# A GEGLU feed-forward layer by Strassen-Winograd: what is loaded beside x's first half, and where four bf16 products stand

## The chip, the cores and the metric

The kernel runs on one core of a Trainium2 chip. A time is the device time of one execution in microseconds; the time before is the median of three runs, 276.03 us (275.87 to 276.15). One further execution was profiled; it took 276.09 us. The engines are TensorE (PE in the profile; PEld is its weight load), VectorE (DVE), ScalarE (ACT), GpSimd (POOL) and SyncE (SP); SP and ScalarE issue the DMAs (SPq, ACTq).

## The reference

```python
def _gelu(x):
    return jax.nn.gelu(x, approximate=True)
def reference(x, w_gate, w_up, w_down):
    return (_gelu(x @ w_gate) * (x @ w_up)) @ w_down
```

x is 32 x 32 x 1024 (1,024 rows of D = 1,024), w_gate and w_up are 1,024 x 3,584, w_down is 3,584 x 1,024, all bf16.

## The kernel before

Every one of the three matrix products is cut in 2 x 2 and done with seven products instead of eight (the Winograd form of Strassen's scheme). The seven products are P1 to P7 in the code's names: `first_products`, `second_products` and so on. In stage 1 the two by two are w_gate's and w_up's columns against the two halves of D (the a's), and x's row halves against the halves of D (the B's: B11 and B21 are the two D halves of the first 512 rows, B12 and B22 those of the last 512, all transposed while they are loaded). F is walked in 28 blocks of 128 columns. P1 and P2 of a block use weights and x as they are loaded, in bf16; the other five use sums of them (S1 to S4, T1 to T4), kept as fp32r. A product is four matmuls of 128 x 128 by 128 x 512.

P1 and P2 of a block together give the gate of the first 512 rows. P1's result is also copied out by ScalarE (E1) and later seeded into another PSUM bank (X), into which P6, P7 and P4 are added in turn: P6, a copy of X by ScalarE (E2), P7, another copy (e3), P4. P5 and P3 go into Y. VectorE makes U1 from Y and e3, H1 from Y and E2, and multiplies gelu's output with them into gT, the input of stage 2. Because the copies are taken between products that go into the same bank, P7 of a block has to wait for the block's E2, and P4 for its e3.

All of this is written out by hand (`tc.manual_schedule()`): each engine and each queue takes its work in the order of the code. The order around the change is this:

- SP starts the transposing load of B11 (L131). ScalarE issues the first part of w_gate tile 0 (L132: the first two of eight row groups of D), then a dummy gelu that brings the activation table in.
- TensorE does ten warm-up products on a constant (L139). Behind the fourth (n = 3) ScalarE copies a few elements and issues three more parts (tile 0's row groups 2 and 3, and the first halves of tiles 1 and 2). Behind the ninth it writes a few elements into B21's place (L147). SP's load of B21 (L148) has to wait for that write, and all later loads of SP stand behind it, in this order: tile 3's first half, the second halves of tiles 0 to 2, half of w_up's first tile, tile 3's second half, tile 4, x's last 512 rows (L155, transposed), tile 5 (L156), the other half of w_up's first tile.
- TensorE: P1 of blocks 0 to 7, P2 of blocks 0 to 7, P1 of 8 and 9, P2 of 8 and 9 (blocks 2c and 2c + 1 use w_gate tile c). Then P5 of blocks 0 and 1 as a pair, P1 of block 10 (`first_products(LEAD)`), P6 of the pair, P1 of block 11, P7 of the pair, P2 of block 10, and P4 and P3 of block 0 and of block 1.
- VectorE: the sums of blocks 0 and 1 as soon as w_up is there, T1 to T4 as soon as x's last 512 rows are there, U1 of blocks 0 and 1 (L258), the sums of block 2, and then the gT and H1 of blocks 0 and 1.
- The loop (L318) then takes one block at a time: P6, the previous block's P4, P5, `ahead()` in most turns, P7, the previous block's P3. `ahead()` does one more P1 and P2 of later blocks; the first call does P1 of block 12 and P2 of block 11.

Stage 2 (L351 on) does the same with gT and w_down. Its last product is the sum of 14 matmuls for each of four row tiles (L502); ScalarE copies each result to SBUF (L506) and it is stored, the last store being issued on ScalarE's own queue.

Of the kernel before, what the change touches and what calls it, by code (L numbers as in the profile page):

```python
# [7 lines left out]
ACT = mybir.ActivationFunctionType  # L8
# [4 lines left out]
def kernel(  # L13
# [18 lines left out]
    nc = tc.nc  # L32
# [10 lines left out]
    DT = D // P  # L43
    KH = DT // 2
    FT = F // P
    NT = N // P
    DB = 512
# [3 lines left out]
    LEAD = 10  # L51
    ALONE = (4, 7, 10, 13, 16, 19, 22, 25)
    KF = FT // 2
    TT = NT // 2
# [28 lines left out]
    def load_gate(c, queue, lo=0, hi=DT):  # L83
        if c not in WG:
            WG[c] = gw.tile([P, DT, 2 * P], bf16, name="gw", tag="gw")
        queue.dma_start(
            out=WG[c][:, lo:hi, :], in_=wg_r[:, lo:hi, 2 * c * P : (2 * c + 2) * P]
        )

    def load_up(c, lo=0, hi=4):  # L90
        if c not in WU:
            WU[c] = uw.tile([P, DT, 4 * P], bf16, name="uw", tag="uw")
        nc.sync.dma_start(
            out=WU[c][:, :, lo * P : hi * P],
            in_=wu_r[:, :, (4 * c + lo) * P : (4 * c + hi) * P],
        )
# [4 lines left out]
    def a11(i):  # L101
        return block(WG, 2, i, 0)

    def a12(i):
        return block(WG, 2, i, 1)
# [18 lines left out]
    def psum_p(name):  # L124
        return psum.tile([P, NB], fp32, name=name, tag="p")

    def psum_q(name):
        return psum.tile([P, NB], fp32, name=name, tag="q")

    with tc.manual_schedule():  # L130
        nc.sync.dma_start_transpose(out=B11, in_=xf[0:NB, 0 : KH * P])  # L131
        load_gate(0, nc.scalar, 0, 2)  # L132
        ones = nc.const_aps.tensor(1.0, [P, NB], bf16)
        warm = [psum_p("warm") for _ in range(4)]
        table = opool.tile([P, 8], bf16, name="table", tag="o")
# [1 line left out]

        for n in range(NWARM):
            nc.tensor.matmul(warm[n % 4], lhsT=ones[:, 0:P], rhs=ones, start=True, stop=True)  # L139
            if n in (3, 8):  # L140
                nc.scalar.activation(table, warm[n % 4][:, 0:8], ACT.Copy)
            if n == 3:
                load_gate(0, nc.scalar, 2, KH)
                load_gate(1, nc.scalar, 0, KH)
                load_gate(2, nc.scalar, 0, KH)
            if n == 8:
                nc.scalar.activation(B21[:, 0, 0:8], table, ACT.Copy)  # L147
# [5 lines left out]
        load_gate(3, nc.sync, KH, DT)  # L153
        load_gate(4, nc.sync)
        nc.sync.dma_start_transpose(out=xt1, in_=xf[NB:N, :])  # L155
        load_gate(5, nc.sync)  # L156
        load_up(0, 2, 4)

        T = {}
# [13 lines left out]
        def early_sums(i, engine=nc.gpsimd):  # L173
            S1[i], S3[i] = weight_tile("s1"), weight_tile("s3")
            engine.tensor_tensor(S1[i], a21(i), a22(i), ALU.add)  # L175
            engine.tensor_tensor(S3[i], a11(i), a21(i), ALU.subtract)  # L176
# [14 lines left out]
        def pair_product(ps, lhs, rhs, first, cuts):  # L191
            for lo, hi in zip(cuts, cuts[1:]):
                for p, l in zip(ps, lhs):
                    for k in range(lo, hi):
                        nc.tensor.matmul(  # L195
                            p,
                            lhsT=l[:, k, :],
                            rhs=rhs[:, k, :],
                            start=(first and k == 0),
                            stop=(k == KH - 1),  # L200
                            skip_group_check=True,
                        )

        def first_products(*blocks, cuts=(0, KH)):
            for i in blocks:
                A[i] = psum_p("a") if 4 <= i < 8 else psum_q("a")
            pair_product([A[i] for i in blocks], [a11(i) for i in blocks], B11, True, cuts)
            for i in blocks:
                if i % 2 == 0:
                    pool, tag = (xpool, "e1") if i == LEAD - 2 else (ring, "ring")  # L210
                    E1[i // 2] = pool.tile([P, 2, NB], fp32, name="e1", tag=tag)
                nc.scalar.activation(E1[i // 2][:, i % 2, :], A[i], ACT.Copy)  # L212

        def second_products(*blocks, cuts=(0, KH)):
            pair_product([A[i] for i in blocks], [a12(i) for i in blocks], B21, False, cuts)
            for i in blocks:
                if i % 2 == 0:
                    GL[i // 2] = half.tile([P, 2, NB], bf16, name="gl0", tag="half")
                nc.scalar.activation(GL[i // 2][:, i % 2, :], A[i], ACT.Gelu_apprx_tanh)

        X, Y, E2, U1, G1 = {}, {}, {}, {}, {}
# [5 lines left out]
        done = LEAD + 2  # L227

        def ahead():
            nonlocal done  # L230
            if done < FT:
                first_products(done)
            second_products(done - 1)
            done += 1

        def sixth_products(*blocks):
            cuts = range(0, KH + 1, 2)
            pair_product([X[i] for i in blocks], [S2[i] for i in blocks], T["T2"], False, cuts)
            for i in blocks:
                E2[i] = epool.tile([P, NB], fp32, name="e2", tag="e2")  # L240
                nc.scalar.activation(E2[i], X[i], ACT.Copy)  # L241
# [9 lines left out]
        def seventh_products(*blocks):  # L251
            cuts = range(0, KH + 1, 2)
            pair_product([X[i] for i in blocks], [S3[i] for i in blocks], T["T3"], False, cuts)
            for i in blocks:
                e3 = epool.tile([P, NB], fp32, name="e3", tag="e3")
                nc.scalar.activation(e3, X[i], ACT.Copy)  # L256
                U1[i] = epool.tile([P, NB], bf16, name="u1", tag="u1")
                nc.vector.tensor_tensor(U1[i], Y[i], e3, ALU.add)  # L258
# [28 lines left out]
        copy_a22(0)  # L287
        second_products(8)
        second_products(9)
        for k in range(KH):  # L290
            nc.scalar.activation(T["B22"][:, k, :], B22[:, k, :], ACT.Copy)
        copy_a22(1)
# [2 lines left out]
        pair_product(  # L295
            [Y[0], Y[1]], [S1[0], S1[1]], T["T1"], True, range(KH + 1)
        )
        first_products(LEAD)
        sixth_products(0, 1)
        first_products(LEAD + 1)  # L300
        seventh_products(0, 1)
        second_products(LEAD)
        early_sums(2, nc.vector)
        second_sum(2)
        seed(2)
# [12 lines left out]
        for i in range(2, FT + 1):  # L318
# [16 lines left out]
            if here and i not in ALONE and done <= FT:  # L335
                ahead()
# [55 lines left out]
        def step(ps, lhs, rhs, j, t, first=False, last=False):  # L392
            for i in range(2):
                nc.tensor.matmul(  # L394
                    ps,
                    lhsT=lhs[:, i, t * P : (t + 1) * P],
                    rhs=rhs[:, i, :],
                    start=(first and j == 0 and i == 0),
                    stop=(last and j == JF - 1 and i == 1),
                    skip_group_check=True,  # L400
                )
# [9 lines left out]
        X = [psum.tile([P, DB], fp32, name="x", tag="p") for t in range(TT)]  # L411
# [90 lines left out]
        for t in range(TT):  # L502
            for j in range(JF):
                step(X[t], SC[j], TC[j], j, t, last=True)
            o_sb = opool.tile([P, DB], bf16, name="o_sb", tag="o")
            nc.scalar.activation(o_sb, X[t], ACT.Copy)  # L506
            queue = nc.sync if t < TT - 1 else nc.scalar
            queue.dma_start(out=of[(TT + t) * P : (TT + t + 1) * P, 0:DB], in_=o_sb)

# [29 lines left out]
```

## Time and profile before

| | before |
|---|---|
| median of 3 runs | 276.03 us (275.87 to 276.15) |
| profiled execution | 276.09 us, of which span 274.3 us |
| PE busy | 268.9 us (98%) |
| PEld busy | 189.3 us (69%) |
| DVE busy | 188.6 us (69%) |
| ACT busy | 138.2 us (50%) |
| POOL busy | 87.2 us (32%) |
| granted TensorE clock, mean | 1.000 |
| DMA | 26.42 MB, mean 96 GB/s |

The span runs from the first to the last instruction of the program. The busy time of TensorE is that of matmuls whose ends are modelled and which overlap; where TensorE loses time is read from the distance of their starts, and from the bracket at the end of a timeline row, which gives the engine's idle time before the row and what ended it. Some matmul records are missing in a trace. In a timeline row the columns are the start, the time from start to end, the engine, the line, the operation, what is written and read with the shapes, and the number of instructions taken together. An SPq or ACTq row is the issue of a DMA; its data moves and lands later.

### The profile page before, as it was taken

How to read it: one execution, taken by the hardware profiler on the slowest of the kernel's cores; microseconds unless marked ns; L12 is line 12 of the kernel's file. 1: busy time of each engine (PE TensorE's matmuls, PEld its weight loads, DVE VectorE, ACT ScalarE, POOL GpSimd, SP SyncE). 2: the span in 40 equal slices, each digit the busy share in tenths (PEclk: the TensorE clock that was granted, in tenths of full speed). 3: DMA queues.
4: the chain of work that ended last, by engine and by line, in shares of the span. 5: the costliest groups of instructions: out<-in, count | busy, mean ns of one | idle time of the engine just before them, and what ended most of it. 6: DMA issues, size and time to landing. Idle time of an engine off the chain costs nothing.

```text
span 274.3 us, 3336 instructions
## 1 busy us (share of the span) xinstructions
PE 268.9 (98%) x1172; PEld 189.3 (69%) x1186; DVE 188.6 (69%) x226; ACT 138.2 (50%) x239; POOL 87.2 (32%) x81
## 2 busy tenths in 40 slices
PE   8999999999999999999999999999999999999995
PEld 2445667768777687776877768764447888888883
DVE  0068974866658666686666866769994999999900
ACT  2678565566556665566655666531100072860311
POOL 0000083845558455584555845600000000000000
PEclk9999999999999999999999999999999999999999
DMA  8999402153400034215360202459602000000221
GB/s 174 280 272 269 155 1 76 51 181 103 128 2 0 0 102 131 76 44 187 97 211 0 76 2 77 114 190 327 215 0 76 2 0 0 1 2 0 97 96 38
DMA packets 41008, 26.42 MB, mean 96 GB/s; under 512 B 9248, under 2 KB 40992, under 8 KB 40992
## 3 DMA queue, kind: packets, MB, share of 16 engines
q1 hardware_dynamic: 39248, 25.30, 31.8%
q10 hardware_dynamic: 1744, 0.92, 1.3%
q8 instruction: 9, 0.15, 0.2%
q14 instruction: 7, 0.06, 0.1%
HBM read 22.02 MB, written 2.10 MB: 88 GB/s over the span
## 4 chain that ended last, share of the span: by engine, by line
PE 96%; DMA 2%; issue 0%; ACT 0%
PE x L195 19%; PE x L394 18%; PE y L115 18%; PE a L195 18%; PE x L115 9%; PE y L394 9%; PE z L394 4%; DMA xt<-in_x_dram 2%; PE y L195 1%; ACT o_sb L506 0%
## 5 line engine op out<-in xcount | busy, mean ns | idle before, releaser
L195 PE MATMUL x<-T,s 128*128 128x512 f32 x224 | 63.4, 407 | 0.0
L195 PEld LDWEIGHTS x<-T,s 128*128 128x128 f32 x224 | 41.6, 188 | 10.9 <-ACT e L241 0.3
L195 PE MATMUL a<-xt,gw 128*128 128x512 bf16 x182 | 44.0, 380 | 1.1 <-DMA xt<-in_x_dram 0.5
L184 POOL TENSOR_TENSOR s<-gw,s 128x512 fp32r<-128x512 bf16 x22 | 26.0, 1184 | 48.4 <-PE y L115 47.7
L258 DVE TENSOR_TENSOR u<-y,e 128x512 bf16<-128x512 f32 x28 | 19.3, 691 | 32.0 <-ACT e L256 31.2
L180 DVE TENSOR_TENSOR s<-s,gw 128x512 fp32r<-128x512 f32 x24 | 34.4, 1434 | 0.0
L195 PEld LDWEIGHTS <-gw 128*128 128x128 bf16 x192 | 17.4, 98 | 24.4 <-issue 5.7
L265 ACT ACTIVATE gl<-h 128x512 bf16<-128x512 bf16 x28 | 17.7, 631 | 28.5 <-DVE h L263 28.5
L245 DVE TENSOR_TENSOR gT<-gl,x 128x512 bf16<-128x512 bf16 x28 | 19.2, 687 | 17.9 <-PE x L115 17.9
L115 PE MATMUL x<-T,c 128*128 128x512 f32 x112 | 30.4, 393 | 0.0
L115 PE MATMUL y<-B,s 128*128 128x512 f32 x112 | 30.2, 391 | 0.0
L175 POOL TENSOR_TENSOR s<-uw 128x512 fp32r<-128x512 bf16 x25 | 29.2, 1167 | 0.0
L115 PE MATMUL y<-T,s 128*128 128x512 f32 x104 | 27.8, 389 | 0.0
L394 PE MATMUL x<-tc,sc 128*128 128x512 f32 x112 | 25.7, 389 | 0.0
L212 ACT ACTIVATE e<-a 128x512 f32<-128x512 f32 x28 | 16.6, 597 | 17.2 <-PE a L195 17.2
L256 ACT ACTIVATE e<-x 128x512 f32<-128x512 f32 x28 | 16.7, 600 | 15.7 <-PE x L195 15.7
L176 POOL TENSOR_TENSOR s<-gw,uw 128x512 fp32r<-128x512 bf16 x21 | 24.5, 1166 | 0.0
L115 PEld LDWEIGHTS x<-T,c 128*128 128x128 f32 x112 | 20.9, 188 | 5.1 <-ACT e L256 0.7
L115 PEld LDWEIGHTS y<-B,s 128*128 128x128 f32 x112 | 21.0, 188 | 4.7
L394 PEld LDWEIGHTS x<-tc,sc 128*128 128x128 f32 x112 | 21.0, 188 | 4.4
L115 PEld LDWEIGHTS y<-T,s 128*128 128x128 f32 x104 | 19.5, 188 | 4.1
L394 PEld LDWEIGHTS <-gT 128*128 128x128 bf16 x112 | 10.9, 98 | 13.3 <-issue 0.3
(57 smaller groups left out, 346.9 us busy)
## 6 DMA issues: line engine op xcount, KB each, us to landing
uw<-in_w_up_dram SPq DMA_DIRECT2D x6, 1024.0 KB, 6.3
gw<-in_w_gate_dram SPq DMA_DIRECT2D x8, 512.0 KB, 3.9
v<-in_w_down_dram SPq DMA_DIRECT2D x5, 512.0 KB, 3.5
v<-in_w_down_dram SPq DMA_DIRECT2D x4, 640.0 KB, 8.2
v<-in_w_down_dram SPq DMA_DIRECT2D x8, 256.0 KB, 4.2
out_dram<-o_sb SPq DMA_DIRECT2D x15, 128.0 KB, 1.7
gw<-in_w_gate_dram SPq DMA_DIRECT2D x5, 256.0 KB, 3.9
uw<-in_w_up_dram SPq DMA_DIRECT2D x2, 512.0 KB, 5.7
```

The costliest lines, as they stand in the source:

```text
L115: nc.tensor.matmul(ps, lhsT=lhs[:, k, :], rhs=rhs[:, k, :], start=(first and k == 0), stop=(k == KH - 1), skip_group_check=True,)
L175: engine.tensor_tensor(S1[i], a21(i), a22(i), ALU.add)
L176: engine.tensor_tensor(S3[i], a11(i), a21(i), ALU.subtract)
L180: nc.vector.tensor_tensor(S2[i], S1[i], a11(i), ALU.subtract)
L184: engine.tensor_tensor(S4[i], a12(i), S2[i], ALU.subtract)
L195: nc.tensor.matmul(p, lhsT=l[:, k, :], rhs=rhs[:, k, :], start=(first and k == 0), stop=(k == KH - 1), skip_group_check=True,)
L212: nc.scalar.activation(E1[i // 2][:, i % 2, :], A[i], ACT.Copy)
L245: nc.vector.tensor_tensor(gT[:, i, 0:NB], GL[i // 2][:, i % 2, :], X[i], ALU.mult)
L256: nc.scalar.activation(e3, X[i], ACT.Copy)
L258: nc.vector.tensor_tensor(U1[i], Y[i], e3, ALU.add)
L265: nc.scalar.activation(G1[i], h1, ACT.Gelu_apprx_tanh)
L394: nc.tensor.matmul(ps, lhsT=lhs[:, i, t * P : (t + 1) * P], rhs=rhs[:, i, :], start=(first and j == 0 and i == 0), stop=(last and j == JF ...
```

## The change

There are four edits.

1. ScalarE no longer issues the first part of w_gate tile 0 ahead of its dummy gelu. All four early parts are issued behind the third warm-up (n = 2) instead of three of them behind the fourth.
2. The load of w_gate tile 5 is two DMAs, the first half of D and the second.
3. Four bf16 products change place. P1 of block 10 stands ahead of P5 of blocks 0 and 1 instead of behind it; P1 of block 11 ahead of P6 instead of behind it; P2 of block 10 ahead of P7 instead of behind it; and P2 of block 11, which was in the loop's first `ahead()`, stands between P7 and P4. The first `ahead()` does P1 of block 12 alone.
4. The copy of the last row tile's result is shared: ScalarE takes the first 256 columns and VectorE the last 256. The store, on ScalarE's queue, waits for both.

```diff
         nc.sync.dma_start_transpose(out=B11, in_=xf[0:NB, 0 : KH * P])
-        load_gate(0, nc.scalar, 0, 2)
...
-            if n in (3, 8):
+            if n in (2, 8):
                 nc.scalar.activation(table, warm[n % 4][:, 0:8], ACT.Copy)
-            if n == 3:
+            if n == 2:
+                load_gate(0, nc.scalar, 0, 2)
                 load_gate(0, nc.scalar, 2, KH)
                 load_gate(1, nc.scalar, 0, KH)
                 load_gate(2, nc.scalar, 0, KH)
...
         nc.sync.dma_start_transpose(out=xt1, in_=xf[NB:N, :])
-        load_gate(5, nc.sync)
+        load_gate(5, nc.sync, 0, KH)
+        load_gate(5, nc.sync, KH, DT)
         load_up(0, 2, 4)
...
             if done < FT:
                 first_products(done)
-            second_products(done - 1)
+            if done > LEAD + 2:
+                second_products(done - 1)
             done += 1
...
         second_products(8)
         second_products(9)
+        first_products(LEAD)
...
         pair_product(
             [Y[0], Y[1]], [S1[0], S1[1]], T["T1"], True, range(KH + 1)
         )
-        first_products(LEAD)
+        first_products(LEAD + 1)
         sixth_products(0, 1)
-        first_products(LEAD + 1)
+        second_products(LEAD)
         seventh_products(0, 1)
-        second_products(LEAD)
+        second_products(LEAD + 1)
         early_sums(2, nc.vector)
...
             o_sb = opool.tile([P, DB], bf16, name="o_sb", tag="o")
-            nc.scalar.activation(o_sb, X[t], ACT.Copy)
+            part = DB if t < TT - 1 else DB // 2
+            nc.scalar.activation(o_sb[:, :part], X[t][:, :part], ACT.Copy)
+            if part < DB:
+                nc.vector.tensor_copy(o_sb[:, part:], X[t][:, part:])
             queue = nc.sync if t < TT - 1 else nc.scalar
```

## The prediction

> **What bounds the kernel now.** I read the page first, then the chain of waits, then the timeline of the first 42 us, then what the DMA queues moved.
>
> ```profile
> span 274.3 us, 3336 instructions
> PE 268.9 (98%) x1172; PEld 189.3 (69%) x1186; DVE 188.6 (69%) x226; ACT 138.2 (50%) x239; POOL 87.2 (32%) x81
> PE 96%; DMA 2%; issue 0%; ACT 0%
> ```
>
> TensorE bounds it, and no product is removed. So only three things can move: the DMA 2% at the head of the chain, the places where TensorE waits, and the copy and store behind its last matmul. The head, by the timeline:
>
> ```profile
> 0.74 1.42 SPq L131 DMA_TRANSPOSE xt<-in_x_dram  x1
> 0.74 0.43 ACTq L86 DMA_DIRECT2D gw<-in_w_gate_dram  x1
> 2.76 1.45 ACTq L86 DMA_DIRECT2D gw<-in_w_gate_dram  x3
> ...
> 5.31 2.37 SPq L148 DMA_TRANSPOSE xt<-in_x_dram  x1
> 5.74 2.53 PE L195 MATMUL a<-xt,gw 128*128 128x512 bf16 x11 [0.54 <-DMA xt<-in_x_dram]
> ...
> 11.07 0.98 PEld L195 LDWEIGHTS <-gw 128*128 128x128 bf16 x6 [0.49 <-DMA gw<-in_w_gate_dram]
> ```
>
> The reader sees x's first half landing at 0.74 + 4.96 = 5.70 (the chain's figure) and the first product at 5.74. The wait at 11.07 is for w_gate tile 3's first half. What the DMA engines did meanwhile, 40 slices of 0.2 us from 0 to 8 us:
>
> ```profile
> DMA  0000000002399999249999999997999999999999
> GB/s 0 0 0 0 0 0 0 0 0 74 110 285 238 251 204 64 44 76 276 291 289 289 294 291 295 334 246 172 300 292 292 282 289 294 289 294 256 233 223 291
> ```
>
> Part one of w_gate moves from 1.8, x from about 2.4. From 2.8 to 3.6 the rate collapses (204, 64, 44, 76), with both in flight; then x runs alone at 290. From about 4.8 the other three ScalarE parts follow, until 7.3, where x's second half starts.
>
> The second place is the end of the setup, 31 to 41 us:
>
> ```profile
> 31.40 1.28 DVE L258 TENSOR_TENSOR u<-y,e 128x512 bf16<-128x512 f32 x2
> 35.00 0.68 DVE L263 TENSOR_TENSOR h<-y,e 128x512 bf16<-128x512 f32 x1
> 36.38 0.69 DVE L263 TENSOR_TENSOR h<-y,e 128x512 bf16<-128x512 f32 x1
> 37.11 0.63 ACT L265 ACTIVATE gl<-h 128x512 bf16<-128x512 bf16 x1 [0.76 <-DVE h L263]
> 37.64 0.61 ACT L187 ACTIVATE c<-uw 128x512 fp32r<-128x512 bf16 x1
> 38.16 0.58 ACT L241 ACTIVATE e<-x 128x512 f32<-128x512 f32 x1
> 38.79 1.67 PEld L195 LDWEIGHTS x<-T,s 128*128 128x128 f32 x8 [0.27 <-ACT e L241]
> 40.24 0.61 ACT L256 ACTIVATE e<-x 128x512 f32<-128x512 f32 x1
> 40.89 0.76 PEld L115 LDWEIGHTS x<-T,c 128*128 128x128 f32 x4 [0.43 <-ACT e L256]
> ```
>
> This is an in-order chain: VectorE's u sums at 31.40, nine VectorE instructions to the second h (ends 37.07), its gelu, the copy of C22, the copy of the sixth product, and only then block 2's seventh product at 38.79. VectorE works without a gap from 22.17, when x's second row half has landed, through T1 to T4, to 37.4. So before the change, this chain starts at a DMA.
>
> **The change part by part.** Small losses are taken between matmul starts: 0.216 us apart in bf16, 0.23 in fp32r; where bf16 turns to fp32r one start takes 0.42. The number of such turns does not change.
>
> 1. *x alone.* 512 KB at 290 GB/s are 1.81 us. From 2.4 that is 4.2, and landing trails the last row by 0.66 (5.04 to 5.70), so x lands near 4.9 instead of 5.70. ScalarE's queue loses its first issue (0.43), so the table load moves up from 1.20 to 0.76; the copy behind the third warm-up starts when that product ends, about 2.3, and the four parts issue from 2.3 to 4.2. Part one now stands behind x. Before, the first part behind x landed 0.49 after it (2.76 + 3.43 = 6.19). So part one lands near 5.4, and TensorE starts near 5.43 instead of 5.74: 0.3 earlier. The ten warm-ups end at 5.0 in both.
>
> 2. *The DMA queue behind it.* 128 KB more follow x (0.45 us at 290), x ends 0.8 to 0.87 earlier: ScalarE's parts end 0.3 to 0.4 earlier. x's second half is still issued at 5.31 (it waits for ScalarE's write at L147 behind the ninth warm-up); the first half took 1.63 from issue to first row, so it can't start before 6.9 instead of 7.25. I take the queue 0.3 earlier from there on. From 9 us it is full until past x's last transpose, so everything in it lands 0.3 earlier. Bounds: 0.6 earlier (a shorter latency when nothing is beside), 0.45 later (the collapse stays, and the 128 KB come on top). Tile 3's first half lands at 10.73 instead of 11.03, against 10.62 when TensorE wants it: a wait of 0.1 stays. TensorE then runs 0.3 ahead to about 22.9.
>
> 3. *One product ahead of P5.* Block 10's first product now comes right behind second product 9 and needs w_gate tile 5, which is why that load is cut in two. Whole, it landed at 20.10 + 4.37 = 24.47, or 2.39 behind x's last transpose (22.08). Its first half: at the earliest 1.14 behind, as tile 3's half landed behind x's second half (11.03 against 9.89); at the latest 1.64 (24.47 less 256 KB at the 350 GB/s of that stretch). I take 1.40, between the two rows, which are equally near: 22.08 - 0.3 + 1.40 = 23.18. TensorE is free at 22.9, so it waits 0.3, and the head start of part 1 is spent. Block 10 starts at 23.23. P5 then finds T1 ready; before, it lost 0.27 there.
>
> 4. *Where the seventh products of blocks 0 and 1 now stand.* From block 10's start: first product 0.65, P5 2.06, first 11 0.66, sixth 2.08, second 10 0.66, a turn: 6.13, so 29.36. Before it was 28.72, with one product fewer ahead. The u sum begins 2.4 later, behind the copy e3: 31.76. Before, e3 was ready at 31.09 and VectorE at 31.40. So the chain now starts 0.36 later, at TensorE, and VectorE idles some 0.6 behind T4.
>
> 5. *One product ahead of P4.* Second product 11 leaves block 2's loop turn and stands ahead of P4. P4 waited for nothing (T4 ends 31.48, its first start is 31.45), so nothing is won there; the matmuls between the seventh products and block 2's seventh become one product fewer (second 10 leaves to the front): 9.95 - 0.86 = 9.09 us. The chain over the same stretch is 2.4 + (38.79 - 31.40 = 7.39) = 9.79. TensorE thus waits 0.7 at block 2's seventh product, which starts at 39.15 instead of 38.79: +0.36.
>
> 6. *Given back.* ScalarE no longer has gelu 11 between that product and its copy e3 (0.5 us in its queue, 39.76). The copy then starts as the product ends, and P4 of block 2 loses 0.06 instead of 0.28: -0.22. From there on the order is the old one, and TensorE has no wait until the end.
>
> 7. *The last copy*, 271.00 to 271.60, with the store issued at 271.62.
>
> ```profile
> 271.00 0.60 ACT o_sb L506
> ```
>
> Half on ScalarE, half on VectorE. ScalarE: 8 columns 0.18 to 0.21, 512 columns 0.60, so 256 take 0.39. VectorE: 512 columns from PSUM 0.69, 1,024 of SBUF 1.22, so 256 take 0.42. The store waits for the slower and a semaphore: -0.15 (bounds -0.2 and, if both reads of one bank collide, 0).
>
> Covered: the extra DMA issue on SP (0.58) delays block 2's w_up (lands 26.3, read at 32.60) and tile 6 (29.1, read at 37.1). GpSimd's sums of block 3 start 0.36 later; their S4 of block 2 ended at 38.43 and is read past 45.
>
> Sum: +0.36 - 0.22 - 0.15 = 0.0. The profiled execution took 276.09 (span 274.3 and 1.8 around it), 0.06 above the median 276.03. So 276.05.
>
> A rule weighed: the Trainium skill, "DMA: Bandwidth & Descriptors", section "Queues, rings and completion order", says that each DMA engine goes round between its queues packet by packet. By it, part one, ready near 3.4, would go between x's rows. The row: from 3.8 to 4.8 us, with ScalarE's next parts issued from 2.76, only x's queue moved (1136 packets, all under 512 B), which speaks against it; the collapse at 2.8 to 3.6 speaks for it.
>
> **The rivals.**
>
> *Slower: the collapse stays.* ScalarE's first part becomes ready about 1.1 us after its issue (0.74 to 1.8 before), so near 3.4, in the middle of x's 1.8 us. If its packets go between x's rows, the 0.8 us are lost again and 0.45 us of part one come behind. The queue is then 0.45 later, tile 5's half lands at 23.93, and the chain of part 4 starts 1.1 later than before: 1.11 - 0.22 - 0.15 = +0.74, 276.8. The same happens if x's second half meets the parts' end and collapses instead; before, it met it at 7.2 at no visible price. It decides above a delay of some 0.25. For it: x's last transpose, which started among loads, also fell to 23 GB/s near 18 us. Against: the full rate from 3.8 to 4.8.
>
> *Faster: VectorE's chain has slack.* If the queue gains 0.6 and tile 5's half lands 1.14 behind, part 4 starts at 31.41, and the sum is 0 - 0.22 - 0.15 = -0.37; the full gain, with no wait at block 2's seventh, would be 0.34 there, 0.28 at P4 and 0.15 at the end: 275.3. Against: nine VectorE instructions in order, none of which the change shortens.
>
> *It does not do what it says*: TensorE starts no earlier, as part one lands late. Then parts 3 to 7 still hold, since tile 5 decides: 276.05 to 276.2.
>
> **How the numbers follow.** No change to the end, 276.05 (275.6 to 276.5 for tile 5's two bounds and a queue gain of 0 to 0.6): 0.5, and 0.05 for the rival that does nothing. The collapse: 0.25, 276.5 to 277.1. Faster: 0.2, 275.0 to 275.5. About 0.2% (0.55 us) is what a measurement of this kernel can tell from no change. That gives faster 0.2, same 0.55, slower 0.25, and a range of 275.3 to 276.9, which leaves out the far ends of both rivals.
>
> **What would show it.** Right: x lands near 4.9 and TensorE starts near 5.4; the rate stays near 290 from 2.4 to 4.2; a TensorE wait for tile 5 near 22.9; no wait for T1; VectorE idle ahead of the u sums; a wait of 0.7 for the sixth product's copy near 39; the store issued 0.45 after the last matmul. Wrong: another collapse in the DMA row, or no growth of the wait near 39.

## The result, and the profile after

The changed kernel took 277.33 us (median of 20 runs, 276.56 to 279.24), the kernel before in the same comparison 276.12 us (275.77 to 276.61, 20 runs). The ratio is 1.0049 (95% interval 1.0037 to 1.0061): 1.2 us are lost, where no change was forecast. The profiled execution of the changed kernel took 276.69 us, so it is one of its quicker ones; what the median adds to it has to come from the experiments.

From the profile's page, the span, the busy times and the chain's shares:

```profile
span 274.9 us, 3341 instructions
PE 268.6 (98%) x1172; PEld 189.5 (69%) x1186; DVE 189.1 (69%) x227; ACT 138.3 (50%) x239; POOL 87.2 (32%) x81
PE 92%; DMA 2%; DVE 2%; ACT 2%; issue 1%; SPq 0%; ACTq 0%
```

TensorE does the same work. What is new is that VectorE and ScalarE stand in the chain with 2% each, where TensorE alone held 96%: TensorE now waits for them somewhere.

The head, by the timeline (start, duration, engine, operation, and in brackets the idle time before and what ended it):

```profile
0.74 1.41 SPq L131 DMA_TRANSPOSE xt<-in_x_dram  x1
2.33 2.02 ACTq L86 DMA_DIRECT2D gw<-in_w_gate_dram  x4
5.32 2.33 SPq L148 DMA_TRANSPOSE xt<-in_x_dram  x1
5.43 5.35 PE L196 MATMUL a<-xt,gw 128*128 128x512 bf16 x24 [0.34 <-DMA gw<-in_w_gate_dram]
11.42 1.25 PE L196 MATMUL a<-xt,gw 128*128 128x512 bf16 x5 [0.64 <-DMA gw<-in_w_gate_dram]
```

and what the DMA engines moved from 0 to 8 us, in slices of 0.2 us:

```profile
DMA  0000000000089999999999999999999999979999
GB/s 0 0 0 0 0 0 0 0 0 0 20 206 255 266 275 246 288 296 288 289 299 250 225 230 261 287 261 284 274 307 320 320 305 305 219 178 232 146 225 247
```

The collapse between 2.8 and 3.6 us is gone, x's first half lands at 4.90, and TensorE starts at 5.43 behind the late first part of w_gate (in this execution just as forecast). But nothing moves before 2.0 us now, and TensorE waits for tile 3's first half until 11.42: by the distance of the matmul starts it loses 0.80 there, and lost 0.16 before. That load landed at 11.38 instead of the forecast 10.73 (11.03 before). The transfers behind x are no earlier: x's last transpose lands at 22.11, against 22.08 before.

The end of the setup:

```profile
23.47 0.58 PEld L196 LDWEIGHTS <-gT 128*128 128x128 bf16 x4 [0.28 <-DMA gT<-in_w_gate_dram]
32.06 1.29 DVE L260 TENSOR_TENSOR u<-y,e 128x512 bf16<-128x512 f32 x2 [0.55 <-ACT e L258]
38.83 0.58 ACT L243 ACTIVATE e<-x 128x512 f32<-128x512 f32 x1
39.46 1.69 PEld L196 LDWEIGHTS x<-T,s 128*128 128x128 f32 x8 [0.86 <-ACT e L243]
41.35 0.76 PEld L115 LDWEIGHTS x<-T,c 128*128 128x128 f32 x4 [0.20 <-ACT e L258]
```

Block 10 waits for tile 5's first half, which landed at 23.43, 1.32 behind x's last transpose. VectorE is idle for 0.55 ahead of the u sums. TensorE's weight load stands 0.86 in front of block 2's seventh product, which starts at 39.46 instead of 38.79. At block 2's P4 the wait is 0.20 instead of 0.43.

The end of the kernel:

```profile
271.44 0.38 ACT L510 ACTIVATE o_sb<-x 128x256 bf16<-128x256 f32 x1 [2.58 <-PE x L397]
271.86 0.42 DVE L512 CAST o_sb<-x 128x256 bf16<-128x256 f32 x1 [11.02 <-ACT o_sb L510]
272.32 0.36 ACTq L514 DMA_DIRECT2D out_dram<-o_sb  x1
```

The two half copies run one behind the other: VectorE's is released by ScalarE's, not by TensorE. From the copy's start to the store's issue it is 0.88 now, and was 0.62 (271.00 to 271.62).

So the books of these two executions are: block 2's seventh product 0.67 later; 231.98 from there to the last copy instead of 232.21, or 0.23 given back; 0.26 more for the copy. That is +0.70, where the span grew by 0.6.

### The profile page after: what moved, and what is told of

It is laid out like the page before. It is cut to its first block, busy times and chain, and to the rows that moved or that the text cites. A ratio compares the mean times of both kernels' runs of the same rounds, so it can differ in the third digit from the quotient of the medians.

```text
span 274.9 us, 3341 instructions
## 1 busy us (share of the span) xinstructions
PE 268.6 (98%) x1172; PEld 189.5 (69%) x1186; DVE 189.1 (69%) x227; ACT 138.3 (50%) x239; POOL 87.2 (32%) x81
## 4 chain that ended last, share of the span: by engine, by line
PE 92%; DMA 2%; DVE 2%; ACT 2%; issue 1%; SPq 0%; ACTq 0%
PE x L196 18%; PE x L397 18%; PE y L115 17%; PE a L196 16%; PE y L397 9%; PE x L115 9%; PE z L397 4%; DMA gw<-in_w_gate_dram 2%; PE y L196 1%; DVE h L265 0%; ACT L135 0%; DVE u L260 0%; ACT gl L267 0%; ACT c L188 0%; ACT e L258 0%
## 5 line engine op out<-in xcount | busy, mean ns | idle before, releaser
L220 ACT ACTIVATE gl<-a 128x512 bf16<-128x512 f32 x28 | 16.7, 597 | 6.7 <-PE a L196 6.6
```

## The experiments

My theory, after the result: edit 3 costs what parts 3 to 5 of the prediction say, the split copy costs instead of gaining, and edit 1 gains nothing and at times loses. Rivals are told where a run is to decide between them. Where an expectation gives a theory a letter, the text around it has it in words. Two landmarks are used throughout: when x's last 512 rows had landed ("x's last transpose"), and when block 2's seventh product started. From that product's start to the end of the profiled time it is 236.9 to 237.6 us in all 19 profiles of the study (237.30 in before, 237.23 in the changed kernel). So a setup is judged by that one start.

### One edit at a time

Edit 1 alone, edits 2 and 3 alone, edit 4 alone, and the changed kernel again beside them:

```
front_only: ScalarE's four parts all behind the third warm-up, nothing else
order_only:
-        load_gate(5, nc.sync)
+        load_gate(5, nc.sync, 0, KH)
+        load_gate(5, nc.sync, KH, DT)
   (and the four bf16 products one place ahead)
tail_only:
-            nc.scalar.activation(o_sb, X[t], ACT.Copy)
+            (the two half copies, as in the change)
```

> The changed kernel once more, for a second profile beside its parts. Its times lie from 276.6 to 279.2 us, those of before from 275.8 to 276.6. Theory A (the loads): what varies is the DMA queue behind x's first half, above all the transposes of x's second half, which meet ScalarE's last parts; then this profile differs from the first one in when w_gate tile 3's first half lands (11.38 us in the first profile, 11.03 before) and in when x's last transpose and tile 5's half land (22.11 and 23.43), and TensorE's order behind that only passes it on. Theory B (the order): the loads land as in the first profile within 0.3 us, and the difference arises between 23 and 42 us. Theory C (the end): the difference arises behind the last matmul.

> Edit 1 alone: all four early parts of w_gate behind the third warm-up, the rest as before. Theory A: slower than before by 0.3 to 1.0 us in the median and spread over 1.5 us or more, as the changed kernel is; in its profile the transposes of x's second half run below 290 GB/s and tile 3's first half lands at 11.3 us or later. Theory B: 0 to -0.3 us, spread as before (0.8 us), since VectorE's chain starts at x's last transpose, which lands at 22.1 in both profiles.

> Edits 2 and 3 alone: tile 5 in two loads and the four products in their new places, the loads at the head as before. By the prediction's steps with x's last transpose at 22.1: tile 5's half lands 1.3 to 1.4 behind it, block 2's seventh product starts 0.6 to 0.7 later than before, 0.2 of it is given back at block 2's P4: +0.4 to +0.5 us, 276.5. Theory A: that, with the narrow spread of before. Theory B: that and more, +0.8 to +1.2 us, with the wide spread, as TensorE now waits directly on a load.

> Edit 4 alone: the last copy shared by ScalarE and VectorE. The changed kernel's profile shows VectorE's half starting only when ScalarE's half is done (271.44 + 0.38, then 271.86 + 0.42), so +0.2 to +0.3 us, 276.3, with the spread of before; had the two halves run together it would be -0.15. Theory C: more than 0.5 us and a wide spread.

| | median, us | ratio (95%) | profiled | x's last transpose | block 2's seventh | between |
|---|---|---|---|---|---|---|
| before | 276.18 | | 276.09 | 22.08 | 38.79 | 16.71 |
| changed again | 277.23 | 1.0048 (1.0030 to 1.0065) | 276.73 | 22.14 | 39.58 | 17.44 |
| edit 1 | 276.78 | 1.0023 (1.0010 to 1.0035) | 276.52 | 22.60 | 39.31 | 16.71 |
| edits 2 and 3 | 276.80 | 1.0024 (1.0015 to 1.0034) | 277.03 | 22.62 | 40.15 | 17.53 |
| edit 4 | 276.38 | 1.0011 (1.0002 to 1.0019) | 276.34 | 22.03 | 38.75 | 16.72 |

(The profiled execution of before is the one shown at the start.) No edit gains. The three differences, +0.60, +0.62 and +0.20, add up to 1.42, a little more than the 1.05 to 1.2 of all together. Edits 2 and 3 cost more than the 0.4 to 0.5 that the prediction's steps give, but not the 0.8 to 1.2 of theory B (the order). The second profile of the changed kernel is again of a quick execution, so it can't tell where the longer ones lose time.

The extra time of edit 4 is the serial copy, which the timeline of that kernel repeats:

```profile
271.02 0.38 ACT L507 ACTIVATE o_sb<-x 128x256 bf16<-128x256 f32 x1 [2.58 <-PE x L394]
271.44 0.42 DVE L509 CAST o_sb<-x 128x256 bf16<-128x256 f32 x1 [10.35 <-ACT o_sb L507]
271.90 0.37 ACTq L511 DMA_DIRECT2D out_dram<-o_sb  x1
```

0.88 from the copy's start to the store's issue, as in the changed kernel; 0.26 more than before.

Edits 2 and 3 show the prediction's mechanism with nothing else in the way: with the old head the seventh product of block 2 starts 17.53 behind x's last transpose, with the old order 16.71 behind it, whatever the head does (16.71 with edit 1 too). Edit 1 leaves that distance alone and moves the landing itself, from 22.08 to 22.60.

### The chain behind the new order

If the wait at block 2's seventh product is the in-order chain of VectorE and ScalarE, then a shorter chain must shorten it. `copy_a22(2)` (the copy of C22, 0.62 on ScalarE) stood in that chain, right ahead of the copy that the seventh product waits for. It moves to an earlier place, alone on the kernel before (copy_early), and together with edits 2 and 3 (order_copy):

```
             fourth_product(i)
+            if i == 0:
+                copy_a22(2)
             third_product(i)
-        copy_a22(2)
```

> The kernel before with one ScalarE instruction moved: block 2's copy of A22 (0.61 us, between the second gelu and the copy of block 2's sixth product) stands behind block 0's P4 instead, where ScalarE idles for 2.8 us. The chain theory (block 2's seventh product waits on ScalarE's order behind VectorE): the copy of the sixth product starts 0.5 us earlier, the waits of 0.27 and 0.43 us at 38.8 and 40.9 shrink to 0 and below 0.2; 0.2 to 0.4 us faster, 275.8 to 276.0. Rival (TensorE's waits there have another cause, the weights' sums or PSUM): no change, within 0.1 us of before.

> Edits 2 and 3 with the same ScalarE instruction moved. Edits 2 and 3 alone took 276.80 (276.55 to 277.44), 0.62 above before; block 2's seventh product started 16.0 us behind tile 5's first half. The chain theory: 15.5 us behind it, the wait of 0.7 us shrinks to 0.2, and the time falls by 0.4 to 0.5 us to 276.3 to 276.4. Rival: no change against edits 2 and 3 alone.

Measured: copy_early 275.75 (0.9992, 0.9983 to 1.0002, so alone the moved copy gains nothing that is clear of the noise), order_copy 276.00 (1.0005, 0.9996 to 1.0013), before 275.95 beside them. The price of the order falls from 0.62 to 0.05 over before, or 0.25 over the kernel with the copy moved alone. The timeline of edits 2 and 3 alone:

```profile
38.46 0.63 ACT L267 ACTIVATE gl<-h 128x512 bf16<-128x512 bf16 x1 [0.76 <-DVE h L265]
39.00 0.61 ACT L188 ACTIVATE c<-uw 128x512 fp32r<-128x512 bf16 x1
39.52 0.58 ACT L243 ACTIVATE e<-x 128x512 f32<-128x512 f32 x1
40.15 1.68 PEld L196 LDWEIGHTS x<-T,s 128*128 128x128 f32 x8 [0.86 <-ACT e L243]
```

and with the copy moved as well:

```profile
34.36 0.62 ACT L188 ACTIVATE c<-uw 128x512 fp32r<-128x512 bf16 x1
...
38.88 0.58 ACT L243 ACTIVATE e<-x 128x512 f32<-128x512 f32 x1
39.51 1.68 PEld L196 LDWEIGHTS x<-T,s 128*128 128x128 f32 x8 [0.34 <-ACT e L243]
```

Between the gelu and the copy e there is no C22 copy any more, and the weight load waits 0.34 instead of 0.86. What is left hangs on tile 5's first half: the seventh product starts 15.99 behind its landing in the one kernel and 15.48 in the other. That the chain sets the wait is shown.

### What edit 1 does to the loads

The forecast of edit 1 was made from one execution, in which x's first half landed at 5.70. The first experiments put that in doubt: with the old head x landed at 5.09 in the kernel with edit 4 alone and at 5.68 in the one with edits 2 and 3. The next runs ask what the loads do. One was to give x a clean way to the end: edit 1, and x's second half issued right behind the first, with the write that held it back (L147) taken out:

```
         nc.sync.dma_start_transpose(out=B11, in_=xf[0:NB, 0 : KH * P])
-        load_gate(0, nc.scalar, 0, 2)
+        nc.sync.dma_start_transpose(out=B21, in_=xf[0:NB, KH * P : D])
...
-            if n == 8:
-                nc.scalar.activation(B21[:, 0, 0:8], table, ACT.Copy)
-        nc.sync.dma_start_transpose(out=B21, in_=xf[0:NB, KH * P : D])
```

> Edit 1 alone, and x's second half is issued right behind its first, without the wait for ScalarE, so that neither meets a load that is under way. Theory A (the queue: a transposing load that starts among loads under way loses 0.3 to 1.1 us, one that starts alone 0.4 to 0.5, and the loss only moved from the first half to the second): the second half moves at 290 GB/s and its last row is in by 6.0 us instead of 9.4; ScalarE's parts follow it, TensorE starts near 7 us instead of 5.7; x's last transpose lands at 21.2 to 21.7 instead of 22.1 to 22.6; spread 0.8 us or less. The time is then set by TensorE's later start: 276.6 to 277.2. Rival (the loss is not in the meeting, a half loses it wherever it stands): the second half's last row comes at 6.5 us or later, x's last transpose lands at 22.0 or later, and the time is over 277.2 with a wide spread.

Measured: 280.31 us (six executions, one of them of 276.78), 1.0123 (1.0082 to 1.0163): 4.4 us slower by the medians and 3.4 by the ratio, the largest effect of the study. x's second half didn't gain at all (11.14 instead of 9.89) and w_gate's first part landed at 9.01. What the DMA engines moved from 0 to 8 us in that kernel:

```profile
DMA  0000000000089999999999999909729999999999
GB/s 0 0 0 0 0 0 0 0 0 0 19 204 287 292 289 291 291 289 289 288 269 259 232 132 145 183 15 44 24 44 140 128 177 169 201 166 198 197 213 271
```

Up to 4.2 us x's rows run alone at 290: the first half's until about 4.1, then the second's. From about 5 us ScalarE's plain parts, issued from 2.3 on, go in between the rows of the second half, and both crawl: 15 to 45 GB/s from 5.2 to 6.0, and mostly under 200 up to 7.6. TensorE started at 9.06, and its matmuls stood 0.427 apart up to 13.3 us, 0.216 from there on, which adds to the loss. So in this execution a transposing load and plain loads that moved together lost rate. They do not always: in the kernel with edit 4 alone 274 packets of x and 105 of part one moved together from 2.4 to 2.8 us at 291 GB/s. My forecast of an early x fell. The run does not decide between the two theories of its expectation, since the second half met loads under way after all.

The Trainium skill, "DMA: Bandwidth & Descriptors", section "Queues, rings and completion order", says that an engine goes round between its queues packet by packet. This rule, which the prediction weighed, stays undecided: the profile before spoke against it from 3.8 to 4.8 us. Here one packet of ScalarE's queue moved beside 667 of SP's, which carries x, from 3.8 to 4.4 us; it was 21 beside 57 from 5.2 to 6.0, and 234 beside 625 from 6.0 to 7.6. So the plain parts stood behind x at first, which speaks against the rule, and later did not wait for x's second half to end, which agrees with it.

Beside it, the changed kernel once more for its profile, since the first was of a quick execution:

> The changed kernel a third time, one look. Its two profiles are of executions of 276.7 us; the median of its times is 277.3. If this one is of 277.2 us or more, theory A expects x's last transpose to land that much later than 22.1, with block 2's seventh product 16.0 us behind tile 5's first half again; the rival, that slow executions lose time elsewhere, expects 22.1 and a TensorE wait in another place.

It took 278.13 us. x landed at 4.87 and its last transpose at 22.78, and something else was late too. In the answer for TensorE's product line between 5 and 10 us, the three numbers are the shortest, the median and the longest duration in ns:

```profile
L196 PEld LDWEIGHTS <-gw x12: 98/151/151, 5.9 to 9.9; 128*128 128x128 bf16 x12
L196 PE MATMUL a<-xt,gw x11: 379/634/634, 5.9 to 9.9; 128*128 128x512 bf16 x11
```

Its matmuls started 0.427 apart until 9.65 us, twice the 0.216 of all later bf16 ones: TensorE came to full speed late. This is called a late full clock below. The granted clock that the profile records reads 1.00 in these stretches too, so only the distance of the starts shows it.

### Is it the gap of TensorE?

With edit 1 TensorE idles between the warm-up and the first product for up to 1.36 us by the brackets (0.34 in the changed kernel's profile, 0.70 where the clock was late; 0.54 in before's). A theory was that this gap delays the full clock and so causes the changed kernel's spread. More or fewer warm-up products close or open the gap:

```
-    NWARM = 10
+    NWARM = 13     (the changed kernel; edit 1 alone)
+    NWARM = 9      (the kernel before)
+    NWARM = 12     (copy_early)
```

> The changed kernel with 13 warm-up products instead of 10. In its one slow profile (278.1 us) TensorE stood idle from about 5.1 to 5.9 and its next nine products were still 427 ns apart, until 9.65 us; in the two faster ones (276.7) the distance was 216 ns from the first product on. Theory D (the clock): the longer gap between the last warm-up and the first product, which waits for w_gate's part one, lets the full clock slip in some executions, and this makes the spread. With the gap filled, no execution is above 277.3 and the median falls to 276.6 to 276.9; what stays above before is the order (0.4 to 0.6) and the end (0.2 to 0.3). Theory A (the loads alone): median 277.3 and spread 1.5 us or more, as without.

> Edit 1 alone with 13 warm-up products instead of 10. Edit 1 alone took 276.78 (276.13 to 277.65). Theory D: 276.1 to 276.3, spread 0.9 us or less. Theory A: 276.7 or more, and the wide spread stays, since the second half of x still meets ScalarE's parts.

> The kernel before with 9 warm-up products instead of 10, nothing else: no load moves, but TensorE's gap ahead of the first product grows by 0.43 us, to about what it is in the changed kernel. Theory D: the wide spread appears, executions above 277 among them, median up by 0.2 to 1.0 us. Theory A: as before within 0.1 us, with the spread of before.

> The kernel before with block 2's copy of A22 moved up (275.75 alone, against 275.95 of before on the same chip) and 12 warm-up products. x's first half lands between 4.9 and 5.7 us in the profiles, and TensorE waits for w_gate tile 3 at 11 us in all of them, so 0.4 us of extra warm-ups cost nothing at the end. Theory D: 0.1 to 0.4 us faster than before, 275.6 to 276.0 where before is 276.1, no execution more than 0.7 us above the median. Theory A: as the moved copy alone, with single executions 0.9 us above the median.

| | median, us | ratio (95%) | TensorE starts | x's last transpose | block 2's seventh |
|---|---|---|---|---|---|
| before, beside them | 276.05 | | | | |
| changed, 13 warm-ups | 277.27 | 1.0055 (1.0037 to 1.0073) | 6.27 | 22.79 | 40.18 |
| edit 1, 13 | 276.70 | 1.0023 (1.0006 to 1.0040) | 6.27 | 23.06 | 39.78 |
| before, 9 | 276.09 | 1.0008 (0.9997 to 1.0020) | 5.00 | 22.04 | 38.77 |
| copy_early, 12 | 275.83 | 0.9994 (0.9986 to 1.0003) | 5.20 | 22.10 | 38.70 |

The warm-ups close the gap (13 of them last until 6.27) and give nothing back: the ratios are those of 10 warm-ups, one of the six executions of the changed kernel with 13 took 278.90, and the theory fell as an account of the price and the spread. The profiles agree that the length of the gap doesn't set the pace: with the longest one, 1.36, the products stood 0.23 and then 0.216 apart at once, and with 13 warm-ups, where TensorE did not idle at all, the distance fell from 0.427 to 0.216 only at 6.7. What stays is x's last transpose, which with edit 1 is on the whole later (the ranges stand in the table of the next section).

### Bytes behind x, or the earlier issue?

Two explanations were left. By the first, edit 1 takes 128 KB out of a time when the DMA engines have nothing else to do and puts them into the full queue behind x; then 0.45 us (128 KB at 290 GB/s) must be lost whatever stands ahead. By the second, the parts' issue at 2.3 instead of 2.76 lets them meet x's rows. So one kernel leaves part one at the head and issues the other three behind the third warm-up (head_kept), and one keeps the old head and adds a load of 128 KB behind the parts that nobody reads (more_bytes):

```
head_kept:
-            if n in (3, 8):            (and n == 3)
+            if n in (2, 8):            (and n == 2)
more_bytes, behind the four parts:
+                nc.scalar.dma_start(
+                    out=gT[:, 5, 0:NB].rearrange("p (b f) -> p b f", f=2 * P),
+                    in_=wg_r[:, 0:2, 0 : 2 * P],
+                )
```

> The kernel before, with the other three parts of w_gate behind the third warm-up instead of the fourth; part one stays ahead of the activation table, beside x. Theory E (the bytes: part one's 128 KB moved from a time when the DMA engines were idle into the full queue): as before within 0.1 us, x's last transpose near 22.1. Theory F (the parts' earlier issue makes them meet x's second half): 0.3 to 0.6 slower, like edit 1 (276.7 to 276.8 where before is 276.1).

> The kernel before, with one more load of 128 KB on ScalarE's queue behind the four parts, into a place that is written later; nothing waits for it. Theory E: 128 KB at 290 GB/s are 0.45 us, so w_gate tile 3 and x's last transpose land 0.4 to 0.5 later and the time is 0.3 to 0.5 above before, with the wider spread. Theory F: as before within 0.1 us, or up to 0.2 above.

Measured, beside 276.29 for the kernel before: head_kept 276.19 (0.9997, 0.9986 to 1.0008), more_bytes 276.83 (1.0016, 1.0004 to 1.0029), with x's last transpose at 22.34 and 22.61. The 128 KB cost 0.54 by the medians and 0.44 by the ratio (0.1 to 0.8 by its interval), about the 0.45 and about what edit 1 costs (0.60), and the earlier issue costs nothing that shows (its interval ends at +0.2). The second explanation fell.

With that, the head can be read over all profiles, eleven with the old head (part one ahead of x), seven with edit 1 (x_whole apart):

| | old head | edit 1 |
|---|---|---|
| x's first half landed | 4.91 to 5.31 in eight, 5.68 to 5.70 in three | 4.87 to 4.98 |
| part one landed | 2.92 to 3.76 | 5.39 to 6.14 |
| TensorE's first product, median | 5.20 (4.95 to 5.74) | 5.94 (5.43 to 6.27) |
| x's last transpose, median | 22.09 (21.82 to 22.62, eight with the same loads) | 22.78 (22.11 to 23.13) |

The mean rate from 0 to 4.9 us fits the first explanation: 155 to 166 GB/s in the eight profiles with the old head and an early x, 131 to 146 with edit 1 (and 131 to 132 in the three with the old head and a late x, which have the collapse). By the medians of the eight and the seven (160 and 143) edit 1 has moved some 80 KB less by then, or 0.3 us at 290 GB/s. The rest of its 0.60 is not located.

The profiles also show which executions with the old head have the collapse. From 2.8 to 3.6 us the packets of x (q1) and of ScalarE's part one (q10), their MB and their share of time are, in before, head_kept and copy_early:

```profile
q1 hardware_dynamic: 262, 0.07, 133.1%
q10 hardware_dynamic: 22, 0.01, 4.5%
...
q1 hardware_dynamic: 711, 0.18, 126.7%
q10 hardware_dynamic: 5, 0.00, 0.9%
...
q1 hardware_dynamic: 906, 0.23, 127.4%
```

In the three profiles in which x landed at 5.68 to 5.70, 15 to 25 packets of ScalarE's queue still moved in that stretch; in head_kept, where x landed at 5.31, 5 did, and in the other seven none. So x is late where the end of part one still moves among its rows. Whether the late end slows x, or x's rows hold up the end, the profiles don't say.

The profile that the prediction was made from is one of the three in which x was late, and the profile of the changed kernel is the one in which part one was soonest. From edit 1 alone (first product):

```profile
6.19 2.12 PE L195 MATMUL a<-xt,gw 128*128 128x512 bf16 x9 [1.36 <-DMA gw<-in_w_gate_dram]
```

It waits for part one, which landed at 6.14, 1.16 behind x.

Last, the changed kernel again:

> The changed kernel once more, one look. Theory E: x's last transpose lands between 22.1 and 23.1, and block 2's seventh product starts 16.0 to 16.1 behind tile 5's first half wherever the first products were 216 ns apart. In an execution of 278 us or more: a late full clock, as in the one profile of 278.1 us, or a transpose that lands after 23.3.

It took 278.00 us. TensorE had its full clock in time; x's last transpose landed at 23.13, and block 10 stood still longer:

```profile
24.85 1.04 PE L196 MATMUL a<-xt,gT 128*128 128x512 bf16 x4 [0.81 <-DMA gT<-in_w_gate_dram]
...
40.77 0.50 PE L196 MATMUL x<-T,s 128*128 128x512 f32 x1 [0.36 <-ACT e L243]
```

Where the transpose lost its time, the DMA engines' rate shows. From 16 to 24 us, in slices of 0.2 us, in before and in this execution:

```profile
GB/s 294 292 297 294 294 285 278 272 255 136 23 74 292 289 289 289 292 289 292 289 289 289 292 289 292 289 289 204 64 44 151 284 302 302 343 353 343 351 341 351
GB/s 287 289 292 294 284 294 292 279 273 282 245 179 102 22 23 17 26 291 288 289 292 289 291 292 288 289 292 289 291 292 288 289 251 74 123 215 284 215 307 312
```

Just before x's last rows run at 290, the rate falls under 30 GB/s for one slice in before and for four here.

So two executions near 278 show two different causes, a late clock and a late transpose; with one profile of each that is a reading and not a test. What makes the one or the other happen wasn't found.

### Can the loads be brought sooner?

Two attempts at a version that beats the kernel before, both with copy_early in them. The first moves tile 3's first half from SP's queue to the end of ScalarE's parts, so that it no longer stands behind x's second half:

```
                 load_gate(2, nc.scalar, 0, KH)
+                load_gate(3, nc.scalar, 0, KH)
...
-        load_gate(3, nc.sync, 0, KH)
```

> The kernel before with block 2's copy of A22 moved up, and tile 3's first half issued by ScalarE behind its other parts instead of by SP behind x's second half. The bytes ahead of x's last transpose stay the same. If TensorE's wait at 11 us (it waits for tile 3 in every profile, 0.2 to 1.6 us) passes to the end, 0.3 to 0.5 us faster than the moved copy alone: 275.3 to 275.6 where before is 276.05. If x's last transpose alone sets the end: as the moved copy alone, 275.8.

275.97 us, 0.9987 (0.9975 to 1.0000), with x's last transpose at 21.71 and block 2's seventh product 16.59 behind it, at 38.30. It is the best ratio of the study, but its interval reaches to 1, and the run doesn't decide between its two expectations. Tile 3's first half was in at 8.58; TensorE then waited 0.29 at 12.04 for tile 0's second half, which landed at 12.00.

The second adds to it x's last transpose between tile 4's two halves, and P5 of blocks 0 and 1 ahead of second products 8 and 9:

```
-        load_gate(4, nc.sync)
+        load_gate(4, nc.sync, 0, KH)
         nc.sync.dma_start_transpose(out=xt1, in_=xf[NB:N, :])
+        load_gate(4, nc.sync, KH, DT)
```

> The kernel before with block 2's copy of a22 half a microsecond sooner, tile 3's first half issued on ScalarE's queue, x's last transpose issued between tile 4's two halves instead of behind both, and P5 of blocks 0 and 1 ahead of second products 8 and 9. If the end follows x's last transpose, as all profiles so far say (the seventh product of block 2 started 16.6 to 16.74 behind it in the old order), then 256 KB less stand ahead of that transpose; at the 290 GB/s of these loads this is up to 0.9 us: it lands near 20.9 instead of 21.7 to 22.1, and the time is 275.3 to 275.8 beside 276.1 to 276.2 for the kernel before. Rival: the half of tile 4 that now lands behind it is what TensorE waits for next, and then the time is that of the kernel before or above it, 276.0 to 276.6.

277.57 us, 1.0040 (1.0025 to 1.0055). The transpose landed at 21.40, 0.68 sooner than in before, and the seventh product of block 2 started at 40.62, 1.83 later. The rival had the sign but not the cause: tile 4's second half landed at 22.80 and nobody waited for it. From the timeline:

```profile
22.33 2.44 PE L196 MATMUL y<-T,s 128*128 128x512 f32 x8 [0.91 <-DVE T L167]
...
27.05 2.18 ACT L297 ACTIVATE B<-xt 128x512 fp32r<-128x512 bf16 x4
...
30.77 2.14 PE L196 MATMUL x<-T,s 128*128 128x512 f32 x8 [0.68 <-ACT e L242]
```

P5 came up so early that it waited 0.91 for T1, work for which second products 8 and 9 had been the cover, and 0.68 more were lost where the copies of B22 now stood ahead of the sixth product's copy on ScalarE. These two are 1.59 of the 2.51 by which the distance from x's last transpose to block 2's seventh product grew (19.22 instead of 16.71); the rest is not located. The distance from x's last transpose to block 2's seventh product holds for one order of products, not for all.

## Why the prediction was wrong

1. *x alone: a step that failed.* "0.3 earlier" for TensorE's start came out in the profiled execution to the hundredth (5.43), and that is luck: the 5.74 it was taken from was one of three late starts among eleven; the old head's median is 5.20, and edit 1's is 5.94. The collapse that the edit removes is absent or short in most executions, as x then lands by 5.31 with part one already in. And the 0.49 from x to part one was the smallest of seven, five of which are 0.9 to 1.2.

2. *The queue behind it: the step that failed most.* "The queue 0.3 earlier" should have been 0.69 later by the medians of x's last transpose, beyond the bound of 0.45 later; the measured price of edit 1 is 0.60. (The ranges overlap, and the changed kernel's own profile has 22.11, so one pair of profiles could not have shown it.) Of that, the 0.45 of the 128 KB was in the text as a term, but set against "x ends 0.8 to 0.87 earlier", which was taken from the one execution. As a typical gain this is nearly nothing: x landed at 5.02 (the median of the other eight) and lands at 4.9. The rival "the collapse stays" had the right sign and the right term (128 KB behind x) by another way: the rows of x's first half did not collapse in any of the seven profiles with edit 1, and the loss was there nevertheless. Nor was the queue "full until past x's last transpose": the rate falls to 23 GB/s near 18 us in the profile before itself, and how long it does so differs between executions.

3. *One product ahead of P5: right.* Tile 5's half was forecast 1.40 behind x's last transpose; it came 1.29 to 1.67 behind in the seven profiles that have it, 1.32 in the changed kernel's. (The start of 0.42 at a turn from bf16 to fp32r, which the prediction lists among the small losses, is none: the start ahead of it stands only 0.03 off, and 0.45 for the two is what one start of 0.216 and one of 0.23 take.)

4 and 5. *The chain: right.* Its working puts the seventh product of block 2 at 17.37 behind x's last transpose (39.15 less 21.78); it was 17.35 in the changed kernel and 17.39 to 17.64 in four of the other five profiles with the new order and the copy in its place (18.17 in the fifth, where TensorE's full clock was late). Its parts hold one by one: 6.14 from block 10 to the seventh products (forecast 6.13), 2.40 to the u sums (2.4), 7.40 from there to block 2's seventh product (7.39). Only the start, 21.78, was wrong.

6. *Given back: right.* -0.22 forecast, -0.23 from the seventh product to the last copy.

7. *The last copy: failed.* -0.15 forecast, with 0 as the bound if the two reads of one bank collide; it is +0.26. The two copies don't run at once: VectorE's waits for ScalarE's in the changed kernel and in the kernel with edit 4 alone. Half a copy takes 0.38 and 0.42 where the whole takes 0.60, so in a row they are longer, and the bound "0" was no bound. Both halves read one PSUM bank and write one tile (o_sb); no run here tells which of the two the wait is for. The Trainium skill, "PSUM — Partial Sum Buffer", section "PSUM bank collisions raise a hardware error", says that two engines may not access one bank over the same partitions at once, two reads included; the wait of VectorE for ScalarE in the timeline agrees with it.

The sum with the measured terms, against medians: +0.64 for the wait at block 2's seventh product (17.35 less 16.71, with no head start from the queue), -0.23, +0.26 for the copy, +0.60 for edit 1, is +1.3; measured is +1.2. The forecast of no change fell on edit 1 and the copy: 0.9 and 0.4 of error, all in one direction.

Open: why the end of part one is late in some executions of the old order, with x's rows collapsing beside it, and not in others, and why the changed kernel spreads wider (276.56 to 279.24 against 275.77 to 276.61).

## What to carry to other kernels

A wait that one profiled execution shows in front of a transfer is a draw, not a constant; before a gain is booked from taking it away, see it in a second profile, and ask where the bytes that are moved out of idle DMA time will stand. A result copy that two engines share from one PSUM bank into one tile ran one half behind the other here; parts in different banks were not tried. Where products are moved ahead in an in-order pipeline, follow the chain of the other engines to the next wait: here it gave that wait to 0.02 us, and one copy of 0.62 moved out of the chain took most of it away.

## What the runs showed of the hardware that was not expected

- A transposing load and plain loads in flight together can lose most of the rate: 15 to 45 GB/s in slices of x_whole, and 44 to 76 in the profile before from 3.0 to 3.6 us, where either alone runs at 290. In the kernel with edit 4 alone they moved together at 291 (2.4 to 2.8 us). What decides this is open.
- Plain parts stood behind x's first half. In the seven profiles with edit 1 part one was issued at 2.33 and its first packet moved at 4.08 to 4.23, when the last of x's rows ran; in the profile before no plain part moved from 3.8 to 4.8 us. In x_whole they went in between the rows of the second half.
- TensorE came to full speed at different times: in all_third the first matmuls ran 0.427 us apart up to 9.65 us after an idle bracket of 0.70, while in the same kernel's other profiles, with brackets of 0.34 to 0.89, the first stood 0.23 apart and all later ones 0.216. With 13 warm-ups and no idleness it was 6.7 us. In x_whole it was 13.3 us, after some 4 us of idleness.
- 128 KB that nobody reads cost 0.54 us of the whole kernel by the medians (0.1 to 0.8 by the ratio's interval) when they stand in the head's full queue.
